# A layer of linear attention and gated MLP: the down projection done by Strassen's method, 7 products for 8

## The chip, the cores and the metric

The kernel runs on one core of a Trainium2 chip. The metric is the device time of one execution in microseconds (us). The profile of an execution has a span about 1.7 us shorter than its device time (792.57 us and 790.9 us for the profiled execution of the kernel before). Where two kernels are compared by time, they are medians; where stages are compared, they are read from the spans of the profiles.

In this text, TensorE is the matrix engine (PE in the profile), PEld its weight loads, VectorE is DVE, ScalarE is ACT, and SP is the engine that issues most DMAs, one after the other, in program order. TensorE's results land in PSUM, in banks (one holds 128 x 512 values here); an *eviction* is the VectorE or ScalarE instruction that reads a finished bank, so that it can be used again. A *residual* is the part of h that is added to the result. The *releaser* of an idle time is what the profile says ended it, and the *granted clock* is the share of the full TensorE clock that the trace records.

## The reference, cut to what matters

```
def reference(A_x, A_wqkv, A_wo, B_x, B_W_gate, B_W_up, B_W_down):
    ...                                   # linear attention block on layernorm(x), 32 heads
    def _B_ref(x, W_gate, W_up, W_down):
        gate = jnp.einsum("bsd,df->bsf", x, W_gate)
        up = jnp.einsum("bsd,df->bsf", x, W_up)
        gate = gate * (gate > 0)
        h = gate * up
        return jnp.einsum("bsf,fd->bsd", h, W_down)
    h = x + _A_ref(_layernorm(x), A_wqkv, A_wo)
    h2 = h + _B_ref(_layernorm(h), B_W_gate, B_W_up, B_W_down)
    return h2
```

2048 tokens (S), width D = 1024, hidden width F = 3584, all bfloat16. The last einsum is the down projection: a 2048 x 3584 matrix times a 3584 x 1024 matrix.

## The kernel before

The MLP is done in two passes of 1024 tokens. In each pass a *gate/up stage* fills `hh` (28 tiles of 128 hidden units x 1024 tokens) and a *down stage* multiplies it by W_down. The gate/up stage already uses the Strassen-Winograd scheme: 14 pairs, each with 7 products for gate and 7 for up, 4 matmuls each, so 56 matmuls per pair where 64 would be needed. For that it forms sums of weight blocks (`t_sums`) and of activation blocks (`s_sums`) on VectorE. The down stage is plain: four rounds of 28 x 4 matmuls.

```
NPASS = 2; TOK = S // NPASS; FTB = 4; NFB = NFT // FTB       # NFT = 28 tiles of F, NFB = 7 chunks
NWS = 4                                                      # W_down ring: 4 chunks of 512 KB
...
def load_wd_next():                                          # next chunk of W_down into the ring
    ...
    rd, c = L // NFB, L % NFB
    dh = rd % ND2
    i = L % NWS
    dma(sl_wd[i], wdring[:, i, :, :], wd_v[:, c * FTB:(c + 1) * FTB, dh * NW:(dh + 1) * NW],
        "ld_wd_%d" % L, writes=[B_wd[i]])
...
def d_round(ps_, hf, dh, banks4, stagger=False, fill=()):    # one round: 512 tokens x 512 columns
    ...
    for j in range(STB):                                     # residuals h, loaded at the round's start
        ...
        dma(sl_hr[k], hres[:, k, :], h_scr[st * P:(st + 1) * P, dh * NW:(dh + 1) * NW], ...)
    def d_mm(ft, j):
        ...
        mm(bank(banks4[j], NW), hh[:, ft, jt * P:(jt + 1) * P], wdring[:, ws, fl, :], ...)
    def d_evac(j):                                           # PSUM + residual -> bf16 -> store
        ...
    for c in range(NFB):
        fts = list(range(c * FTB, (c + 1) * FTB))
        if c == NFB - 1:                                     # last chunk: bank by bank
            for j in range(STB):
                for ft in fts:
                    d_mm(ft, j)
                d_evac(j)
        else:
            for ft in fts:
                for j in range(STB):
                    d_mm(ft, j)
        load_wd_next()
        if fill:
            fill.pop(0)()                                    # pass 0: layernorm of the second half
```

All DMAs, loads and stores alike, are issued by SP in program order (`dma` adds to the program of "sp"). A DMA that must wait for a semaphore therefore holds every DMA behind it.

## Time and profile before

| what | value | view |
|---|---|---|
| device time | 793.66 us median (793.29 to 795.0; 3 runs) | times |
| span | 790.9 us | page |
| TensorE busy | 99%, 3791 matmuls | page, part 1 |
| VectorE busy | 55% | page, part 1 |
| chain that ended last | 95% matmul | page, part 4 |
| down projection | 896 matmuls | groups |

From the page of the kernel before, part 1 (busy time of each engine) and part 4 (the chain that ended last):

```profile
PE 779.6 (99%) x3791; PEld 360.0 (46%) x3791; DVE 434.4 (55%) x900; ACT 237.3 (30%) x394; POOL 30.5 (4%) x60
...
PE 95%; DVE 2%; issue 1%; DMA 1%; SPq 1%; ACT 0%; POOL 0%; DVEq 0%; POOLq 0%
```

The 99% alone is not relied on here: the Trainium skill ("Perfetto Trace Analysis", Identifying the Most-Contended Engine) says that matmul busy time is a poor measure of how close a kernel is to its peak, because matmuls are pipelined. The chain is the stronger evidence: 95% of the span is one matmul after another.

From the groups of instructions of the kernel before, each shape on its own; columns are line, engine, operation, tiles, shapes, count, busy us, mean ns of one, and idle time before with its releaser:

```profile
L504 PE MATMUL ps<-RW,RAB 128*128 128x512 bf16 x896 | 193.9, 380 | 1.1 <-DMA RW<-in_B_W_down_dram 1.1
L777 DVE TENSOR_TENSOR RE<-wring,RE 128x512 f16<-128x512 bf16 x108 | 45.5, 421 | 1.8
L777 DVE TENSOR_TENSOR RE<-wring 128x512 f16<-128x512 bf16 x108 | 40.6, 418 | 0.0
L894 DVE TENSOR_TENSOR RX<-ps,RX 128x512 bf16<-128x512 f32 x32 | 21.8, 690 | 127.3 <-PE ps L504 106.6
L838 DVE TENSOR_TENSOR RAB<-ps,RAB 128x512 bf16<-128x512 f32 x28 | 19.4, 692 | 109.9 <-PE ps L504 109.9
```

The first line is the down projection: 896 matmuls, of which the busy sum of 193.9 us gives 0.216 us each (the 380 ns is from start to end of one, and they overlap). The two L777 lines are what a weight sum of 128 x 512 costs on VectorE, the L894 line what an eviction of one PSUM bank costs. L838 is the first eviction of each gate/up pair: VectorE is idle 3.9 us (109.9 / 28) before it on average. That is the room in which new sums can hide.

The two down stages of the kernel before, in TensorE's timeline (start us, duration us, engine, line, operation, count, idle before and releaser). First pass 0:

```profile
423.74 38.15 PE L504 MATMUL ps<-RW,RAB 128*128 128x512 bf16 x176
463.04 58.94 PE L504 MATMUL ps<-RW,RAB 128*128 128x512 bf16 x272 [1.15 <-DMA RW<-in_B_W_down_dram]
521.81 1.89 PE L504 MATMUL ps<-hnT,wring 128*128 128x512 bf16 x8
...
691.03 96.86 PE L504 MATMUL ps<-RW,RAB 128*128 128x512 bf16 x448
```

Pass 1 (last line) has 448 matmuls in one block: from the first start to the last, 447 steps, it is 96.86 less the last one's 0.38 us, so 0.2158 us each, and 448 of them are 96.69 us. The Trainium skill ("TensorE: Matmul & The Clock Gate", Part 2, Step-by-step) gives 512/2.4 + about 2.5 ns, measured 215.7 ns, from one matmul to the next; this trace has 215.8 ns and agrees. Pass 0 takes 521.81 - 423.74 = 98.07 us, 1.38 us more, because of one gap, shown as 1.15 us. The reason for it is in SP's timeline of the same kernel:

```profile
450.81 2.12 SPq L437 DMA_DIRECT2D out_dram<-RX  x4
453.03 0.39 SPq L437 DMA_DIRECT2D RW<-in_B_W_down_dram  x1
453.52 1.24 SPq L441 DMA_TRANSPOSE hnT<-RE  x1
454.85 0.53 SPq L437 DMA_DIRECT2D RE<-h_scr  x1
455.43 1.92 SPq L437 DMA_DIRECT2D RX<-h_scr  x4
457.44 0.38 SPq L437 DMA_DIRECT2D RW<-in_B_W_down_dram  x1
```

Between two loads of W_down (453.03 and 457.44 us) stand a transpose, a load of the layernorm's input and four loads of residuals, all behind four stores that wait for their evictions. The second of these loads lands 5.55 us after it was issued, just too late, as the chain of waits has it (start us, us, what):

```profile
457.44 5.55 DMA RW<-in_B_W_down_dram
```

That flight is itself longer than the 3.7 us median of the W_down loads of this kernel.

### The profile page before, as it was taken

The numbers are of one execution on the slowest core, as the hardware profiler recorded it, in microseconds if no ns is written. First come the engines' busy times: TensorE is split into PE (matmuls) and PEld (weight loads), VectorE is DVE, ScalarE is ACT, GpSimd is POOL, SyncE is SP. The second block draws the span as 40 slices with busy tenths as digits, with TensorE's granted clock in tenths as the row PEclk, the third lists the DMA queues.
The fourth block names the chain that finished last, engine by engine and source line by source line (L and its number), as shares of the span: only waits on it lengthen the run. The fifth ranks groups of instructions, "written<-read, shape, count | busy, mean of one in ns | idle before, by whom it ended". The sixth has DMA issues, their size and how long they took to land.

```text
span 790.9 us, 10017 instructions
## 1 busy us (share of the span) xinstructions
PE 779.6 (99%) x3791; PEld 360.0 (46%) x3791; DVE 434.4 (55%) x900; ACT 237.3 (30%) x394; POOL 30.5 (4%) x60
## 2 busy tenths in 40 slices
PE   8999999999979999999999999999999999999998
PEld 4444444444434444444444444444444444444443
DVE  7445535799986667576573632145756756501111
ACT  4333333323210544544542000025445454400000
POOL 2000000001500000000000100000000000000000
PEclk9999999999999999999999999999999999999999
DMA  9677400155564532331335997633323222046562
GB/s 314 189 188 180 112 17 1 27 125 146 143 134 123 170 107 62 98 107 54 107 96 170 240 266 238 203 117 106 93 68 106 73 89 80 0 133 204 196 211 81
DMA packets 160128, 102.37 MB, mean 129 GB/s; under 512 B 50384, under 2 KB 153040, under 8 KB 160080
## 3 DMA queue, kind: packets, MB, share of 16 engines
q1 hardware_dynamic: 160080, 101.73, 44.8%
q8 instruction: 30, 0.49, 0.3%
q14 instruction: 18, 0.15, 0.1%
HBM read 81.79 MB, written 8.39 MB: 114 GB/s over the span
## 4 chain that ended last, share of the span: by engine, by line
PE 95%; DVE 2%; issue 1%; DMA 1%; SPq 1%; ACT 0%; POOL 0%; DVEq 0%; POOLq 0%
PE ps L504 95%; DMA RW<-in_B_W_down_dram 1%; DVE RO L679 1%; DVE RC L761 0%; SPq L437 0%; DVE RX L894 0%; PE ps L573 0%; DVE hsb L703 0%; SPq L441 0%; DVE rden L672 0%; DVE dtmp L668 0%; DVE RX L540 0%; ACT RX L538 0%; DVE RAB L543 0%; POOL hsb L399 0%
## 5 line engine op out<-in xcount | busy, mean ns | idle before, releaser
L504 PE MATMUL ps<-RW,RAB 128*128 128x512 bf16 x896 | 193.9, 380 | 1.1 <-DMA RW<-in_B_W_down_dram 1.1
L504 PE MATMUL ps<-RC,RE 128*128 128x512 f16 x672 | 154.2, 380 | 0.0
L504 PEld LDWEIGHTS ps<-RW,RAB 128*128 128x128 bf16 x896 | 87.4, 98 | 107.3 <-DMA RW<-in_B_W_down_dram 1.8
L788 ACT ACTIVATE ps<-ps 128x512 f32<-128x512 f32 x112 | 65.2, 582 | 187.9 <-PE ps L504 187.3
L504 PE MATMUL ps<-RAB 128*128 128x512 bf16 x512 | 113.4, 380 | 0.9 <-ACT RAB L576 0.7
L504 PE MATMUL ps<-hnT,wring 128*128 128x512 bf16 x448 | 105.9, 380 | 0.0
L504 PEld LDWEIGHTS ps<-RC,RE 128*128 128x128 f16 x672 | 65.7, 98 | 79.4
L894 DVE TENSOR_TENSOR RX<-ps,RX 128x512 bf16<-128x512 f32 x32 | 21.8, 690 | 127.3 <-PE ps L504 106.6
L788 ACT ACTIVATE RO<-ps 128x512 f32<-128x512 f32 x112 | 66.9, 597 | 54.5 <-PE ps L504 54.5
L838 DVE TENSOR_TENSOR RAB<-ps,RAB 128x512 bf16<-128x512 f32 x28 | 19.4, 692 | 109.9 <-PE ps L504 109.9
L504 PEld LDWEIGHTS ps<-RAB 128*128 128x128 bf16 x512 | 49.3, 98 | 57.7 <-ACT RAB L576 0.9
L504 PEld LDWEIGHTS ps<-hnT,wring 128*128 128x128 bf16 x448 | 43.8, 98 | 52.9
L538 ACT ACTIVATE RX<-ps 128x512 bf16<-128x512 f32 x64 | 38.0, 594 | 89.1 <-PE ps L504 62.4
L504 PE MATMUL ps<-RW,RO 128*128 128x512 bf16 x256 | 59.2, 387 | 0.4 <-DMA RO<-RO 0.4
L504 PE MATMUL ps<-RAB,RC 128*128 128x512 bf16 x256 | 58.7, 379 | 0.0
L540 DVE TENSOR_SCALAR RX<-RX 128x512 bf16<-128x512 bf16 x64 | 19.5, 305 | 61.3 <-ACT RX L538 61.2
L504 PE MATMUL ps<-hnT,RE 128*128 128x512 bf16 x224 | 52.9, 380 | 0.0
L504 PE MATMUL ps<-RC,wring 128*128 128x512 f16 x224 | 52.9, 380 | 0.0
L788 ACT ACTIVATE RAB<-ps 128x512 bf16<-128x512 f32 x56 | 33.4, 597 | 62.0 <-PE ps L504 62.0
L777 DVE TENSOR_TENSOR RE<-wring,RE 128x512 f16<-128x512 bf16 x108 | 45.5, 421 | 1.8
L845 DVE TENSOR_TENSOR RO<-ps,RO 128x512 f32<-128x512 f32 x56 | 38.7, 692 | 5.5 <-ACT RO L788 5.4
L777 DVE TENSOR_TENSOR RE<-wring 128x512 f16<-128x512 bf16 x108 | 40.6, 418 | 0.0
(59 smaller groups left out, 486.7 us busy)
## 6 DMA issues: line engine op xcount, KB each, us to landing
RW<-in_B_W_down_dram SPq DMA_DIRECT2D x56, 512.0 KB, 3.7
wring<-in_B_W_gate_dram SPq DMA_DIRECT2D x28, 512.0 KB, 3.8
wring<-in_B_W_up_dram SPq DMA_DIRECT2D x28, 512.0 KB, 4.8
RAB<-in_A_wqkv_dram SPq DMA_DIRECT2D x8, 512.0 KB, 7.7
RX<-in_A_x_dram SPq DMA_DIRECT2D x16, 256.0 KB, 3.1
h_scr<-hsb SPq DMA_DIRECT2D x16, 256.0 KB, 3.3
RX<-h_scr SPq DMA_DIRECT2D x32, 128.0 KB, 3.7
out_dram<-RX SPq DMA_DIRECT2D x32, 128.0 KB, 1.7
```

The source lines that it names most:

```text
L504: lambda e: e.matmul(out_ap, lhsT, rhs, start=start, stop=stop, skip_group_check=skip),
L538: PL.add("act", lambda e: e.activation(out=Et[:, k, 0:w], in_=src, func=ACTF.Exp), reads=[B_bank[b]], writes=[B_E[k]], name=name + "_exp")
L540: PL.add("dve", lambda e: e.tensor_scalar(out=E2t[:, k, 0:w], in0=Et[:, k, 0:w], scalar1=1.0, scalar2=1e-6, op0=ALU.min, op1=ALU.add), rea ...
L679: lambda e, nbk=nbk, g0=g0, ng=ng: e.tensor_tensor(out=osb[:, k, g0 * P:(g0 + ng) * P].rearrange("p (g h e) -> p g h e", g=ng, e=Dh), in0= ...
L777: PL.add(eng, lambda e: e.tensor_tensor(out=Tring[:, k, j], in0=in0, in1=in1, op=ALU.subtract), reads=reads, writes=[B_T[k][j]], name="T%d ...
L788: PL.add("act", lambda e: e.activation(out=dst, in_=src, func=func), reads=reads, writes=writes, name=name)
L838: PL.add("dve", lambda e: e.tensor_tensor(out=hh[:, f1, 0:SBW], in0=bank(BA[1]), in1=r11[:, rr, :], op=ALU.mult), reads=[B_bank[BA[1]], B_ ...
L845: PL.add("dve", lambda e, w=w: e.tensor_tensor(out=ftmp[:, 4 + w, :], in0=bank(BF_[w]), in1=ftmp[:, 2 + w, :], op=ALU.add), reads=[B_bank[ ...
L894: PL.add("dve", lambda e: e.tensor_tensor(out=outst[:, k, :], in0=bank(banks4[j], NW), in1=hres[:, k, :], op=ALU.add), reads=[B_bank[banks ...
```

## The change

The intent: do the down stage with the same Strassen-Winograd scheme, 7 products for 8. Call the activations A (rows: two blocks of 512 tokens, t; columns: even and odd tiles of F, k) and the weights B (rows: even and odd tiles of F; columns: the two halves of D). With

- D1 = A10 + A11, D2 = D1 - A00, D3 = A00 - A10, D4 = A01 - D2 (activation sums, FP16),
- T0 = B01 - B00, T1 = B11 - T0, T2 = B11 - B01, T3 = B10 - T1 (weight sums, FP16),

seven products replace eight: C00 = A00 B00 + A01 B10; U = A00 B00 + D2 T1; V = U + D3 T2; C11 = V + D1 T0; C10 = V + A11 T3; C01 = U + D1 T0 + D4 B11.

The weight sums are the same for both passes. They are formed once, by VectorE, during pass 0's gate/up stage, and put into a DRAM scratch (`t_scr`), from which the down stages load them. Most of the activation sums overwrite `hh` in place.

```diff
-    FTB = 4
-    NFB = NFT // FTB
+    FTB = 2
+    NFB = NPAIR // FTB
+    t_scr = nc.dram_tensor("t_scr", [4 * P, NPAIR * NW], f16).ap()
...
-        NWS = 4
+        NWS = 8                       # ring: 8 chunks of 256 KB
+        NHR = 8                       # residual buffers, 4 before
+        NWR = 2
...
+        WSRC = [("b", 0, 0), ("t", 1), ("b", 1, 0), ("t", 2), ("t", 0), ("t", 3), ("b", 1, 1)]
...
+        def wd_sums(q):               # weight sums of pair q, then to DRAM
+            ...
+            add(0, wb(0, 1), wb(0, 0), [B_wraw[k]])
+            add(2, wb(1, 1), wb(0, 1), [B_wraw[k]])
+            add(1, wb(1, 1), wsum[:, k, 0, :], [B_wraw[k], B_wsum[k][0]])
+            add(3, wb(1, 0), wsum[:, k, 1, :], [B_wraw[k], B_wsum[k][1]])
+            if q + NWR < NPAIR:
+                load_wraw(q + NWR)
+            dma(sl_ws[k], t_v[:, :, q, :], wsum[:, k, :, :], "st_wt_%d" % q, ...)
...
+        def down_pass(ps_, fill):
+            XB, YB = [0, 1, 2, 3], [4, 5, 6, 7]          # two sets of four PSUM banks
+            ...
+            seq = [                                      # banks, activations, FP16?, start, eviction
+                (XB, a_hh(0, 0), False, True, e_s1),     # A00 B00
+                (YB, a_16(0, 0), True, True, e_u),       # D2 T1
+                (XB, a_hh(1, 0), False, False, e_11),    # A01 B10
+                (YB, a_16(0, 1), True, True, e_v),       # D3 T2
+                (XB, a_d1(), True, True, e_22),          # D1 T0
+                (YB, a_hh(1, 1), True, True, e_21),      # A11 T3
+                (XB, a_16(1, 0), False, False, e_12),    # D4 B11
+            ]
+            ...                        # 7 chunks per product; in the last chunk bank by bank,
+                                       # 2 matmuls per bank, then evac(j)
+                    if c == 1 and pi in (1, 3, 4, 5):    # residuals load in mid-product
+                        ld_h(...)
+                    if fill and n[0] % 3 == 2:           # late layernorm at every third chunk
+                        fill.pop(0)()
...
+        wt_at = {0: [0], 1: [1, 2], 2: [3, 4]}           # weight sums per gate/up pair of pass 0
+        for q in range(3, 12):
+            wt_at[q] = [q + 2]
```

A caution on the values: the down projection adds at most 0.001 to outputs of standard deviation 0.078 (reckoned by running the reference with W_down set to zero). The comparison with the reference therefore hardly sees the down projection. What speaks for the change's correctness is its algebra, written out above, not that comparison.

More of the change, by code (lines that the diff above doesn't have):

```diff
@@ L189, in bass_sequential_preLN__linear_attn_block__glu_gated_reglu__prompt_kernel @@
     wu_v = B_W_up.rearrange("(dc p) f -> p dc f", p=P)
-    wd_v = B_W_down.rearrange("(ft p) c -> p ft c", p=P)
+    wd_v = B_W_down.rearrange("(q k p) c -> p k q c", k=2, p=P)
+    t_scr = nc.dram_tensor("t_scr", [4 * P, NPAIR * NW], f16).ap()
+    t_v = t_scr.rearrange("(o p) (q c) -> p o q c", p=P, c=NW)
     h_scr = nc.dram_tensor("h_scr", [S, D], bf16).ap()
@@ L221, in bass_sequential_preLN__linear_attn_block__glu_gated_reglu__prompt_kernel @@
         o0 = NFT * TOK
+        hh16 = RAB[:, 0:NFT * TOK].bitcast(f16).rearrange("p (a b) -> p a b", a=NFT)
+        dsum = RAB[:, o0:o0 + 4 * SBW].bitcast(f32).rearrange("p (a b) -> p a b", a=2)
         r11 = RAB[:, o0:o0 + 2 * SBW].rearrange("p (a b) -> p a b", a=2)
@@ L232, in bass_sequential_preLN__linear_attn_block__glu_gated_reglu__prompt_kernel @@
         wdring = RW[:].rearrange("p (s f c) -> p s f c", s=NWS, f=FTB)
+        wdring16 = RW[:].bitcast(f16).rearrange("p (s f c) -> p s f c", s=NWS, f=FTB)
+        wraw = RW[:, 0:NWR * 2 * D].rearrange("p (s k c) -> p s k c", s=NWR, k=2)
+        wsum = RW[:, NWR * 2 * D:NWR * 2 * D + NWR * 4 * NW].bitcast(f16).rearrange("p (s o c) -> p s o c", s=NWR, o=4)
         hnT = sb("hnT", [P, NDC, TOK], bf16)
@@ L253, in bass_sequential_preLN__linear_attn_block__glu_gated_reglu__prompt_kernel @@
         wring = sb("wring", [P, NWG, NDC, 2 * P], bf16)
-        xn = sb("xn", [P, NXN, D], bf16)
-        hsb = sb("hsb", [P, NHS, D], bf16)
+        RXH = sb("RXH", [P, (NXN + NHS) * D], bf16)
+        xn = RXH[:, 0:NXN * D].rearrange("p (a b) -> p a b", a=NXN)
+        hsb = RXH[:, NXN * D:(NXN + NHS) * D].rearrange("p (a b) -> p a b", a=NHS)
+        D1 = RXH[:].bitcast(f16).rearrange("p (q t) -> p q t", t=SBW)
         RX = sb("RX", [P, 2 * NPH * NW + NX2 * D], bf16)
@@ L260, in bass_sequential_preLN__linear_attn_block__glu_gated_reglu__prompt_kernel @@
         x2 = RX[:, o0:o0 + NX2 * D].rearrange("p (a b) -> p a b", a=NX2)
-        hres = RX[:, 0:NOS * NW].rearrange("p (a b) -> p a b", a=NOS)
-        outst = RX[:, NOS * NW:2 * NOS * NW].rearrange("p (a b) -> p a b", a=NOS)
+        hres = RX[:, 0:NHR * NW].rearrange("p (a b) -> p a b", a=NHR)
+        outst = RX[:, NHR * NW:(NHR + NOS) * NW].rearrange("p (a b) -> p a b", a=NOS)
         zeros_t = hsb[:, 0, 0:512]
@@ L303, in bass_sequential_preLN__linear_attn_block__glu_gated_reglu__prompt_kernel @@
         sl_wd = slots("dwd_", NWS)
-        sl_hr = slots("dhr_", NOS)
+        sl_hr = slots("dhr_", NHR)
+        sl_wr = slots("dwr_", NWR)
+        sl_ws = slots("dws_", NWR)
         sl_out = slots("dout_", NOS)
@@ L347, in bass_sequential_preLN__linear_attn_block__glu_gated_reglu__prompt_kernel @@
         B_hh = [bufs("hh%d_" % i, 2) for i in range(NFT)]
-        B_s7 = bufs("s7_", 2)
-        B_sc = bufs("sc_", 2)
-        B_c21 = bufs("c21_", 2)
-        B_c22 = bufs("c22_", 2)
+        B_f = bufs("f_", 8)
+        B_s7, B_sc, B_c22, B_c21 = B_f[0:2], B_f[2:4], B_f[4:6], B_f[6:8]
+        B_U, B_V = B_f[0:4], B_f[4:8]
         B_r11 = bufs("r11_", 2)
         B_r12 = bufs("r12_", 2)
+        B_dsum = [B_r11, B_r12]
         B_wd = bufs("wd_", NWS)
-        B_hres = bufs("hres_", NOS)
+        B_hres = bufs("hres_", NHR)
+        B_wraw = bufs("wraw_", NWR)
+        B_wsum = [bufs("wsum%d_" % i, 4) for i in range(NWR)]
+        B_tscr = bufs("tscr_", NPAIR)
+        B_D1 = bufs("D1_", NPAIR)
         B_outst = bufs("outst_", NOS)
@@ L372, in bass_sequential_preLN__linear_attn_block__glu_gated_reglu__prompt_kernel @@
             b_.over = B_wq
+        for b_ in B_wraw + flat(B_wsum):
+            b_.over = B_wo
         for b_ in B_wd:
-            b_.over = B_wo
-        for b_ in B_s7 + B_sc + B_c21 + B_c22:
+            b_.over = B_wraw + flat(B_wsum)
+        for b_ in B_D1:
+            b_.over = B_xn + B_hs
+        for b_ in B_f:
             b_.over = B_o + B_oT
@@ L487, in bass_sequential_preLN__linear_attn_block__glu_gated_reglu__prompt_kernel, with load_wraw, wb, add @@
         wd_next = [0]
-        NROUND = NPASS * 2 * ND2
+        WSRC = [("b", 0, 0), ("t", 1), ("b", 1, 0), ("t", 2), ("t", 0), ("t", 3), ("b", 1, 1)]
         def load_wd_next():
             L = wd_next[0]
-            if L >= NROUND * NFB:
+            if L >= NPASS * 7 * NFB:
                 return
             wd_next[0] += 1
-            rd, c = L // NFB, L % NFB
-            dh = rd % ND2
             i = L % NWS
-            dma(sl_wd[i], wdring[:, i, :, :], wd_v[:, c * FTB:(c + 1) * FTB, dh * NW:(dh + 1) * NW],
-                "ld_wd_%d" % L, writes=[B_wd[i]])
+            c = L % NFB
+            src = WSRC[(L // NFB) % 7]
+            if src[0] == "b":
+                dma(sl_wd[i], wdring[:, i, :, :],
+                    wd_v[:, src[1], c * FTB:(c + 1) * FTB, src[2] * NW:(src[2] + 1) * NW],
+                    "ld_wd_%d" % L, writes=[B_wd[i]])
+            else:
+                dma(sl_wd[i], wdring16[:, i, :, :], t_v[:, src[1], c * FTB:(c + 1) * FTB, :],
+                    "ld_wt_%d" % L, reads=B_tscr[c * FTB:(c + 1) * FTB], writes=[B_wd[i]])
+        def load_wraw(q):
+            k = q % NWR
+            dma(sl_wr[k], wraw[:, k, :, :], wd_v[:, :, q, :], "ld_wraw_%d" % q, writes=[B_wraw[k]])
+        def wd_sums(q):
+            k = q % NWR
+            def wb(r, h):
+                return wraw[:, k, r, h * NW:(h + 1) * NW]
+            def add(o, in0, in1, reads):
+                PL.add("dve", lambda e: e.tensor_tensor(out=wsum[:, k, o, :], in0=in0, in1=in1, op=ALU.subtract),
+                       reads=reads, writes=[B_wsum[k][o]], name="WT%d_%d" % (o, q))
+            add(0, wb(0, 1), wb(0, 0), [B_wraw[k]])
[4 more added lines that the diff above has]
+                load_wraw(q + NWR)
+            dma(sl_ws[k], t_v[:, :, q, :], wsum[:, k, :, :], "st_wt_%d" % q, reads=B_wsum[k], writes=[B_tscr[q]])
         def mm(out_ap, lhsT, rhs, start, stop, reads, bbuf, name, skip=False):
@@ L788, in ident_act, with hh_sums, strassen_pair @@
             PL.add("act", lambda e: e.activation(out=dst, in_=src, func=func), reads=reads, writes=writes, name=name)
-        def strassen_pair(ps_, q, fill):
+        def hh_sums(q):
+            f1, f2 = 2 * q, 2 * q + 1
+            PL.add("dve", lambda e: e.tensor_tensor(out=D1[:, q, :], in0=hh[:, f1, SBW:2 * SBW],
+                                                    in1=hh[:, f2, SBW:2 * SBW], op=ALU.add),
+                   reads=[B_hh[f1][1], B_hh[f2][1]], writes=[B_D1[q]], name="D1_%d" % q)
+            PL.add("dve", lambda e: e.tensor_tensor(out=hh16[:, f1, SBW:2 * SBW], in0=hh[:, f1, 0:SBW],
+                                                    in1=hh[:, f1, SBW:2 * SBW], op=ALU.subtract),
+                   reads=[B_hh[f1][0]], writes=[B_hh[f1][1]], name="D3_%d" % q)
+        def strassen_pair(ps_, q, fill, mid):
             Lg = (ps_ * NPAIR + q) * 2
@@ L833, in strassen_pair @@
             fillin(2)
+            for f_ in mid:
+                f_()
             for w in range(2):
@@ L868, in strassen_pair, with ld_h, tt, put @@
             load_w_next()
+        hr_ctr = [0]
         os_ctr = [0]
-        def d_round(ps_, hf, dh, banks4, stagger=False, fill=()):
-            rd = (ps_ * 2 + hf) * ND2 + dh
-            kk = []
-            for j in range(STB):
-                st = ps_ * TPP + hf * STB + j
+        U_ = [ftmp[:, j, :] for j in range(STB)]
+        V_ = [ftmp[:, STB + j, :] for j in range(STB)]
+        def down_pass(ps_, fill):
+            XB, YB = [0, 1, 2, 3], [4, 5, 6, 7]
+            hr = {}
+            def ld_h(blk, dh):
+                for j in range(STB):
+                    st = ps_ * TPP + blk * STB + j
+                    k = hr_ctr[0] % NHR
+                    hr_ctr[0] += 1
+                    hr[(blk, dh, j)] = k
+                    dma(sl_hr[k], hres[:, k, :], h_scr[st * P:(st + 1) * P, dh * NW:(dh + 1) * NW],
+                        "ld_h_%d_%d" % (st, dh), reads=[B_hscr[st]], writes=[B_hres[k]])
+            def tt(dst, in0, in1, reads, writes, name, op=ALU.add):
+                PL.add("dve", lambda e: e.tensor_tensor(out=dst, in0=in0, in1=in1, op=op), reads=reads,
+                       writes=writes, name=name)
+            def put(blk, dh, j, in0, in1, reads):
+                st = ps_ * TPP + blk * STB + j
@@ L877, in d_round @@
                 k = os_ctr[0] % NOS
                 os_ctr[0] += 1
-                kk.append(k)
-                dma(sl_hr[k], hres[:, k, :], h_scr[st * P:(st + 1) * P, dh * NW:(dh + 1) * NW],
-                    "ld_h_%d_%d" % (st, dh), reads=[B_hscr[st]], writes=[B_hres[k]])
-            def d_mm(ft, j):
-                c, fl = ft // FTB, ft % FTB
-                ws = (rd * NFB + c) % NWS
-                jt = hf * STB + j
-                mm(bank(banks4[j], NW), hh[:, ft, jt * P:(jt + 1) * P], wdring[:, ws, fl, :],
-                   ft == 0, ft == NFT - 1, [B_hh[ft][hf], B_wd[ws]], B_bank[banks4[j]],
-                   "d_%d_%d" % (rd, ft))
@@ L891, in d_evac @@
-            def d_evac(j):
-                st = ps_ * TPP + hf * STB + j
-                k = kk[j]
-                PL.add("dve", lambda e: e.tensor_tensor(out=outst[:, k, :], in0=bank(banks4[j], NW),
-                                                        in1=hres[:, k, :], op=ALU.add),
-                       reads=[B_bank[banks4[j]], B_hres[k]], writes=[B_outst[k]], name="out_%d_%d" % (st, dh))
+                tt(outst[:, k, :], in0, in1, reads, [B_outst[k]], "out_%d_%d" % (st, dh))
                 dma(sl_out[k], ov[st * P:(st + 1) * P, dh * NW:(dh + 1) * NW], outst[:, k, :],
@@ L898, in d_evac, with hv @@
                     "st_%d_%d" % (st, dh), reads=[B_outst[k]])
-            for c in range(NFB):
-                fts = list(range(c * FTB, (c + 1) * FTB))
-                if c == NFB - 1:
-                    for j in range(STB):
-                        for ft in fts:
-                            d_mm(ft, j)
-                        d_evac(j)
-                else:
-                    for ft in fts:
-                        for j in range(STB):
-                            d_mm(ft, j)
-                load_wd_next()
-                if fill:
-                    fill.pop(0)()
+            def hv(blk, dh, j):
+                k = hr[(blk, dh, j)]
+                return hres[:, k, :], B_hres[k]
@@ new lines, in e_s1, with e_u, e_11, e_v @@
+            def e_s1(j):
+                ident_act(U_[j], bank(XB[j]), [B_bank[XB[j]]], [B_U[j]], "ds1")
+            def e_u(j):
+                tt(U_[j], bank(YB[j]), U_[j], [B_bank[YB[j]]], [B_U[j]], "dU")
+            def e_11(j):
+                h, hb = hv(0, 0, j)
+                put(0, 0, j, bank(XB[j]), h, [B_bank[XB[j]], hb])
+            def e_v(j):
+                tt(V_[j], bank(YB[j]), U_[j], [B_bank[YB[j]], B_U[j]], [B_V[j]], "dV")
+            def e_22(j):
+                h, hb = hv(1, 1, j)
+                k = j % 2
+                tt(dsum[:, k, :], bank(XB[j]), V_[j], [B_bank[XB[j]], B_V[j]], B_dsum[k], "d22")
+                put(1, 1, j, dsum[:, k, :], h, B_dsum[k] + [hb])
@@ new lines, in e_21, with e_12, add_h, a_hh @@
+            def e_21(j):
+                put(1, 0, j, bank(YB[j]), V_[j], [B_bank[YB[j]], B_V[j]])
+            def e_12(j):
+                put(0, 1, j, bank(XB[j]), U_[j], [B_bank[XB[j]], B_U[j]])
+            def add_h(dst, bufs_, blk, dh):
+                for j in range(STB):
+                    h, hb = hv(blk, dh, j)
+                    tt(dst[j], dst[j], h, [hb], [bufs_[j]], "dh")
+            def a_hh(k, t):
+                return (lambda q, j: hh[:, 2 * q + k, (t * STB + j) * P:(t * STB + j + 1) * P]), \
+                       (lambda q: B_hh[2 * q + k][t])
@@ new lines, in a_16, with a_d1, d2, d4 @@
+            def a_16(k, t):
+                return (lambda q, j: hh16[:, 2 * q + k, (t * STB + j) * P:(t * STB + j + 1) * P]), \
+                       (lambda q: B_hh[2 * q + k][t])
+            def a_d1():
+                return (lambda q, j: D1[:, q, j * P:(j + 1) * P]), (lambda q: B_D1[q])
+            def d2(q):
+                tt(hh16[:, 2 * q, 0:SBW], D1[:, q, :], hh[:, 2 * q, 0:SBW], [B_D1[q]], [B_hh[2 * q][0]],
+                   "D2_%d" % q, op=ALU.subtract)
+            def d4(q):
+                tt(hh16[:, 2 * q + 1, 0:SBW], hh[:, 2 * q + 1, 0:SBW], hh16[:, 2 * q, 0:SBW], [B_hh[2 * q][0]],
+                   [B_hh[2 * q + 1][0]], "D4_%d" % q, op=ALU.subtract)
@@ new lines, in down_pass, with d_mm @@
+            seq = [
[7 more added lines that the diff above has]
+            ]
+            n = [0]
+            for pi, (bk, (af, ab), w16, start, evac) in enumerate(seq):
+                for c in range(NFB):
+                    ws = ((ps_ * 7 + pi) * NFB + c) % NWS
+                    wr = wdring16 if w16 else wdring
+                    last = c == NFB - 1
+                    def d_mm(fl, j):
+                        q = c * FTB + fl
+                        mm(bank(bk[j]), af(q, j), wr[:, ws, fl, :], start and q == 0, q == NPAIR - 1,
+                           [ab(q), B_wd[ws]], B_bank[bk[j]], "d%d_%d_%d" % (pi, ps_, q), skip=True)
+                    if last:
+                        for j in range(STB):
+                            for fl in range(FTB):
+                                d_mm(fl, j)
+                            evac(j)
+                    else:
+                        for fl in range(FTB):
+                            for j in range(STB):
+                                d_mm(fl, j)
+                    load_wd_next()
+                    if pi == 0:
+                        d2(2 * c)
+                        d2(2 * c + 1)
+                    if pi == 2 and c >= 1:
+                        d4(2 * c - 2)
+                        d4(2 * c - 1)
+                    if pi == 3 and c == 0:
+                        d4(2 * NFB - 2)
+                        d4(2 * NFB - 1)
+                    if c == 1 and pi in (1, 3, 4, 5):
+                        ld_h(*{1: (0, 0), 3: (1, 1), 4: (1, 0), 5: (0, 1)}[pi])
+                    if pi == 5 and c == 2:
+                        add_h(V_, B_V, 1, 0)
+                    if pi == 6 and c == 2:
+                        add_h(U_, B_U, 0, 1)
+                    if fill and n[0] % 3 == 2:
+                        fill.pop(0)()
+                    n[0] += 1
@@ L1005, in bass_sequential_preLN__linear_attn_block__glu_gated_reglu__prompt_kernel @@
                 s_sums()
-        for _ in range(NWS):
-            load_wd_next()
+        for q in range(NWR):
+            load_wraw(q)
+        wt_at = {0: [0], 1: [1, 2], 2: [3, 4]}
+        for q in range(3, 12):
+            wt_at[q] = [q + 2]
         for p_ in range(NPASS):
@@ L1014, in bass_sequential_preLN__linear_attn_block__glu_gated_reglu__prompt_kernel @@
                     fill = fill + t_sums(nxt) + t_sums(nxt + 1)
-                strassen_pair(p_, q, fill)
-                assert not fill or q == NPAIR - 1 or len(fill) <= 0
-            rounds = [(hf, dh) for hf in range(2) for dh in range(ND2)]
-            for i, (hf, dh) in enumerate(rounds):
-                late = []
-                if p_ + 1 < NPASS and i < 2:
-                    for t in range(i * NFB, (i + 1) * NFB):
-                        late.append(lambda t=t: late_ln(t))
-                if p_ + 1 < NPASS and i == 2:
-                    late.append(s_sums)
-                d_round(p_, hf, dh, [0, 1, 2, 3] if i % 2 == 0 else [4, 5, 6, 7], fill=late)
-                assert not late
+                if q > 0:
+                    hh_sums(q - 1)
+                mid = []
+                if p_ == 0:
+                    for x in wt_at.get(q, []):
+                        mid.append(lambda x=x: wd_sums(x))
+                strassen_pair(p_, q, fill, mid)
+                if p_ == 0 and q == 12:
+                    for _ in range(NWS):
+                        load_wd_next()
+            assert not fill
+            hh_sums(NPAIR - 1)
+            late = []
+            if p_ + 1 < NPASS:
+                for t in range(TPP + 2):
+                    late.append(lambda t=t: late_ln(t))
+                late.append(s_sums)
+            down_pass(p_, late)
+            assert not late
         PL.finalize(eng_sems)
```

## The prediction

> **What bounds the kernel now.** TensorE. The page's part 1 has it busy 99% of a 790.9 us span, the chain that ended last is 95% matmul, and the granted clock is 0.998. In the second pass's down projection (timeline of TensorE, 691.03 us on) 448 matmuls follow each other without a gap and end at 787.7 us: 96.7 us, so 0.216 us each (the groups' 380 ns is pipelined latency). The Trainium skill ("VectorE: DVE Perf Modes", the TRN2 errata) gives 215 ns for a 512-column matmul; this trace agrees. VectorE is busy 55%.
>
> **Removed.** The down projection has 896 matmuls (group RW,RAB). Seven products for eight leave 784: 112 fewer, 112 x 0.216 = 24.2 us, all critical, 12.1 us per pass. Gate/up products on FP16 sums already run at this pitch. Also removed is a 1.15 us TensorE gap at 463 us (queue held by residual loads, W_down tile late); residuals now have twice the buffers and load mid-product.
>
> **Added, mostly hidden.**
> - Weight sums, 14 x 4 VectorE ops of 128x512 to FP16. The gate/up weight sums of this shape take 418 to 421 ns, so 1.7 us per pair, in pass 0 only. Activation sums: 4 per pair and pass at about 0.42 us, half of them in the gate/up stage (0.84 us per pair). A pair takes 12.1 us (56 matmuls); VectorE idles about 3.8 us of it before its first eviction (line 838: 53.6 us idle over 14 pairs). 0.84 + 1.7 = 2.5 us fits. Pairs 1 and 2 carry two sets (4.2 us), overrunning by about 0.4 us; the bank they delay is next needed over 5 us later.
> - Evictions in the down stage: about 28 FP32 ops from PSUM or SBUF at 0.69 us plus 8 residual adds per pass, some 25 us, and 12 us of in-place sums, in 84.6 us. Products alternate between two sets of four banks, so each eviction has a 12 us window. No wait expected.
> - DMA: ring loads keep their rate (256 KB per 1.73 us against 512 KB per 3.46 us); 14 raw loads and 14 stores of 512 KB are new, in pass 0.
>
> **What I expect to be given back.**
> - Pass 0, about 1.5 us: the layernorm of the second half ends later in the down stage; its sums (4 x 1.22 us) wait for the last transpose (4.5 us in flight) and come just before the longest eviction, 8 x 0.69 us (product 5). Its stores stand in the DMA queue ahead of the weight loads. I reckon the queue blocked some 9 us against a ring of 8 chunks (13.8 us) and 4 us of flight, so the first tile of product 7 lands 1 to 2 us late.
> - Tail, 0.7 us: the last chunk gives 0.43 us of matmuls per bank (0.86 before), less than one 0.69 us eviction, so evictions queue after the last matmul.
>
> **Sum.** 793.7 - 24.2 - 1.2 + 1.5 + 0.7 = 770.5 us. Range 767.5 to 774.5. Faster by over 2% (below 777.8): 0.94; within 2%: 0.05; slower: 0.01.
>
> **What would show it.** 784 matmuls in the down groups at an unchanged 0.216 us pitch; pass 1's down stage 84.6 us without gaps; pass 0's at 86 us with its one gap before product 7, released by a W_down or scratch DMA; gate/up stages still 12.1 us per pair; VectorE about 65% busy.
>
> **What would make it wrong.** Weight sums pushing VectorE late enough to hold gate/up banks (pairs over 12.1 us); a longer or repeated stall of the DMA queue in the down stage; a lower granted clock.

## More of the kernel before

(Idle time counts from the end of a matmul, 0.38 us after its start, when the next could have started 0.16 us earlier; so a gap costs about 0.16 us more than it shows.)

## The result and the profile after

| | before | after |
|---|---|---|
| device time, median | 793.47 us (791.29 to 795.0, 4 runs) | 768.12 us (767.77 to 768.56, 4 runs) |
| ratio after to before | | 0.968, 95% interval 0.966 to 0.971: faster |
| span of the profile | 790.9 us | 766.2 us |

The 793.47 us are the three runs from above and a fourth of 791.29 us. A ratio is the mean time of one kernel's fast runs over that of the other's of the same rounds, so it is not quite the ratio of the medians quoted.

From the page of the changed kernel, parts 1 and 4:

```profile
PE 751.8 (98%) x3615; PEld 349.6 (46%) x3679; DVE 519.6 (68%) x1108; ACT 241.4 (32%) x402; POOL 30.6 (4%) x60
...
PE 95%; DVE 3%; issue 1%; ACT 1%; DVEq 0%; POOL 0%; ACTq 0%; POOLq 0%
```

The bound has not moved. The weight loads are 3679, exactly 112 fewer than 3791. (The matmul records show 3615; this trace lacks some of them, so the weight loads are the count to use.) VectorE does 208 more operations.

The changed kernel's TensorE timeline, down stage of pass 0, then of pass 1:

```profile
423.88 48.51 PE L553 MATMUL ps<-RW,RAB 128*128 128x512 bf16 x221
472.23 12.25 PE L553 MATMUL ps<-RW,RXH 128*128 128x512 f16 x56
484.31 12.25 PE L553 MATMUL ps<-RW,RAB 128*128 128x512 f16 x56
496.90 12.03 PE L553 MATMUL ps<-RW,RAB 128*128 128x512 bf16 x54 [0.34 <-DVE RX L949]
508.77 1.89 PE L553 MATMUL ps<-hnT,wring 128*128 128x512 bf16 x8
...
677.99 48.51 PE L553 MATMUL ps<-RW,RAB 128*128 128x512 bf16 x221
726.33 12.25 PE L553 MATMUL ps<-RW,RXH 128*128 128x512 f16 x56
738.42 24.34 PE L553 MATMUL ps<-RW,RAB 128*128 128x512 f16 x110
```

Products follow each other at 12.08 to 12.09 us (472.23 to 484.31, 726.33 to 738.42), which is 56 x 0.2158, whatever their types. Pass 1 has no gap. Pass 0 has one before product 7. It is shown as 0.34 us, but two of product 7's 56 records are missing (x54), the first among them; the stage loses 84.89 - 392 x 0.2158 = 0.28 us (unrounded).

Putting the boundaries of the stages of both spans side by side (each is the start of the first matmul of the next stage) shows where the 24.6 us came from (the last two rows with the unrounded spans):

| stage | before, us | after, us | saved |
|---|---|---|---|
| attention, up to the first gate/up matmul | 254.53 | 254.67 | -0.14 |
| gate/up, pass 0 | 169.21 | 169.21 | 0.00 |
| down, pass 0 | 98.07 | 84.89 | 13.18 |
| gate/up, pass 1 | 169.22 | 169.22 | 0.00 |
| down, pass 1, with the tail | 99.83 | 88.25 | 11.58 |
| span | 790.86 | 766.24 | 24.62 |

The gate/up stage of pass 0, which now carries all weight sums and half of the activation sums, has not grown by a hundredth of a microsecond. The gate/up and down stages of pass 0 by windows, for the busy time of each engine (columns: window, its length, then busy us and count of PE, PEld, DVE, ACT, POOL, then granted clock, DMA share and GB/s). Before:

```profile
254.50:423.70 169.20, 169.20 (x785) 76.65 (x784) 111.48 (x224) 82.74 (x140) 0.00 (x0) 1.00 0.32 95
423.70:521.80 98.10, 96.95 (x449) 43.66 (x448) 33.05 (x61) 0.00 (x0) 4.39 (x8) 1.00 0.82 237
```

After:

```profile
254.60:423.90 169.30, 168.56 (x773) 76.73 (x785) 141.10 (x306) 82.75 (x140) 0.00 (x0) 1.00 0.59 182
423.90:508.80 84.90, 84.35 (x389) 38.31 (x393) 54.67 (x110) 2.07 (x4) 4.58 (x8) 1.00 0.88 250
```

In pass 0's gate/up stage VectorE went from 111.5 to 141.1 us of 169.2, and the DMA engines from 32% to 59%. Both are still off the critical path. The margin is thin in the pairs with two sets of weight sums. The pairs 1 and 2 of the changed kernel, and then a pair with one set:

```profile
267.00:279.00 12.00, 11.95 (x56) 5.46 (x56) 11.76 (x28) 5.91 (x10) 0.00 (x0) 1.00 0.76 239
279.20:291.30 12.10, 12.05 (x57) 5.47 (x56) 11.72 (x27) 5.91 (x10) 0.00 (x0) 1.00 0.86 269
...
303.40:315.50 12.10, 12.05 (x56) 5.49 (x56) 10.17 (x23) 5.91 (x10) 0.00 (x0) 1.00 0.58 175
```

VectorE is busy 11.7 to 11.8 us of some 12 in the first two, 10.2 in the third (the kernel before: 7.9 to 8.0 in each).

The gap before product 7: VectorE's timeline of the changed kernel first, then SP's.

```profile
482.78 2.36 DVE L810 TENSOR_TENSOR RC<-hnT 128x2048 f16<-128x2048 bf16 x2 [3.95 <-DMA hnT<-RE]
485.18 1.23 DVE L810 TENSOR_TENSOR RC<-RC,hnT 128x2048 f16<-128x2048 f16 x1
486.44 1.23 DVE L810 TENSOR_TENSOR RC<-hnT,RC 128x2048 f16<-128x2048 bf16 x1
487.58 0.68 DVE L949 TENSOR_TENSOR RAB<-ps,RO 128x512 f32<-128x512 f32 x1
```

```profile
478.91 1.24 SPq L463 DMA_TRANSPOSE hnT<-RE  x1
480.25 2.90 SPq L459 DMA_DIRECT2D RW<-t_scr  x4
489.07 4.48 SPq L459 DMA_DIRECT2D out_dram<-RX  x4
493.65 1.45 SPq L459 DMA_DIRECT2D RW<-in_B_W_down_dram  x3
```

VectorE waits 3.95 us for the last transpose of the late layernorm, then does the four sums (L810) before it can evict product 5 (from 487.58 us on). Product 5's four stores stand in SP's program ahead of the next weight load. SP has issued its last load at 483.15 us (480.25 + 2.90) and issues the next one only at 493.65 us. That one is the first chunk of product 7, which TensorE wants at 496.4 us. The profile puts the gap down to an eviction (`DVE RX L949`). The eviction running at that moment is product 6's, and no operand or bank of product 7 depends on it, so I took it for a late tile; experiments e3 and e4 decide. The kept trace of this run says so too: the tile landed 2.9 us after its issue, at 496.55 us, and TensorE's queue holds a wait for that load's semaphore which ended at 496.58 us. TensorE's instructions after it wait for VectorE's semaphore as well, and the first matmul's record is missing, which may be why the profile named VectorE. In e5, e6, e7 and e9, which have the same queue, that wait also ended 0.03 us after the tile's landing.

### The profile page after: what moved, and what is told of

It reads as the page before. It is cut to its first block, busy times and chain, and to the rows that moved or that the text cites. A ratio compares the mean times of both kernels' runs of the same rounds, so it can differ in the third digit from the quotient of the medians.

```text
span 766.2 us, 10114 instructions
## 1 busy us (share of the span) xinstructions
PE 751.8 (98%) x3615; PEld 349.6 (46%) x3679; DVE 519.6 (68%) x1108; ACT 241.4 (32%) x402; POOL 30.6 (4%) x60
## 4 chain that ended last, share of the span: by engine, by line
PE 95%; DVE 3%; issue 1%; ACT 1%; DVEq 0%; POOL 0%; ACTq 0%; POOLq 0%
PE ps L553 94%; ACT RX L587 1%; DVE RAB L592 1%; DVE RO L728 1%; DVE RC L810 0%; DVE RX L589 0%; DVE RX L949 0%; PE ps L622 0%; DVE RXH L752 0%; DVE rden L721 0%; DVE dtmp L717 0%; DVE RE L592 0%; DVEq L1187 0%; POOL RXH L421 0%; ACT RAB L625 0%
## 5 line engine op out<-in xcount | busy, mean ns | idle before, releaser
L553 PE MATMUL ps<-RW,RAB 128*128 128x512 f16 (+1 forms) x662 | 145.2, 379 | 0.8 <-DVE RX L949 0.3
L553 PEld LDWEIGHTS ps<-RW,RAB 128*128 128x128 bf16 (+1 forms) x672 | 65.7, 98 | 79.7 <-DVE RX L949 0.6
L837 ACT ACTIVATE RO<-ps 128x512 f32<-128x512 f32 x120 | 71.0, 597 | 76.7 <-PE ps L553 54.5
L553 PE MATMUL ps<-hnT,RE 128*128 128x512 bf16 x196 | 47.0, 379 | 1.5
L553 PEld LDWEIGHTS ps<-RW,RO 128*128 128x128 bf16 x256 | 25.2, 99 | 30.8 <-issue 2.3
```

What stands on the lines that cost most here:

```text
L553: lambda e: e.matmul(out_ap, lhsT, rhs, start=start, stop=stop, skip_group_check=skip),
L837: PL.add("act", lambda e: e.activation(out=dst, in_=src, func=func), reads=reads, writes=writes, name=name)
```

## Experiments

Twelve kernels were run. "Queue edit" below means that the output stores are issued from ScalarE's DMA queue.

### e1: an eighth product put back

```diff
-        WSRC = [..., ("t", 3), ("b", 1, 1)]
+        WSRC = [..., ("t", 3), ("b", 1, 1), ("b", 1, 1)]
...
-                (XB, a_16(1, 0), False, False, e_12),
+                (XB, a_16(1, 0), False, False, None),
+                (XB, a_16(1, 0), False, False, e_12),
```

Its output is wrong, which doesn't matter for the time. Product 7 is done twice, so the matmul count is that of the kernel before.

> An eighth product is put back: product 7 runs twice in each pass (wrong values, same matmul count, 896, as the kernel before; everything else as changed). Theory (the gain is the matmul count, the rest nets to about nothing): 768.1 + 112 x 0.216 = 792.3 us, within about 1.5 us of the kernel before (793.5). Rival (a good part of the 25 us came from something else, such as the reordered queue or other banks): it stays well under 790 us, and the second pass's down stage shows it.

Measured: 792.43 us (791.12 to 794.59), the kernel before in the same rounds 793.05 us; ratio 1.000, interval 0.998 to 1.002: the same. What the change saves is its 112 matmuls; everything else that it adds, moves and repairs nets to nothing within that interval of 0.2% (1.6 us). (e1 has gaps of its own before and within the added products: its down stage of pass 0 takes 98.45 us, 1.8 us over 448 x 0.2158.)

### e2 to e4: the gap before product 7

e2 does the second half's activation sums twice, which makes VectorE later by about 4.8 us at the crucial place and changes nothing else:

```diff
-                late.append(s_sums)
+                late.append(lambda: (s_sums(), s_sums()))
```

> The activation sums of the second half (4 VectorE ops, 4.9 us), which stand before product 5's eviction in pass 0, are done twice (result unchanged). Theory: VectorE's lateness holds the stores, the stores hold the DMA queue, and the weight tile for product 7 is late by the same 4.9 us: the gap before product 7 grows from 0.35 to about 5.2 us, and the time to about 773.0 us. Rival (the slot was luck, there is slack of several us left): under 770 us.

e3 is the queue edit; e4 is both edits together.

```diff
-            return PL.add("sp", lambda e: e.dma_start(dst_ap, src_ap), ...)
+            return PL.add(eng, lambda e: e.dma_start(dst_ap, src_ap), ...)
...
-                    "st_%d_%d" % (st, dh), reads=[B_outst[k]])
+                    "st_%d_%d" % (st, dh), reads=[B_outst[k]], eng="act")
```

> The output stores are issued from ScalarE's DMA queue instead of the common one, so that weight loads no longer stand behind them. Theory (the gap of 0.35 us before product 7 is a late weight tile): the gap goes, about 767.8 us. Rival (the gap is what the profile names, a wait for VectorE's eviction): the gap stays at 0.35 us and the time at 768.1.

> Both edits: sums twice and stores on ScalarE's queue. VectorE is as late as with the sums twice alone, but the weight loads are free. Late-tile theory: no gap before product 7, about 767.8 us. Rival (VectorE holds TensorE directly, through a bank or an operand): about 5 us of gap and 773 us, as without the queue edit.

| | median, us | down stage of pass 0 in the profile, us (84.6 without a gap) |
|---|---|---|
| changed kernel | 768.12 | 84.89 |
| e2, sums twice | 774.86 (772.96 to 775.44) | 90.92 |
| e3, queue edit | 767.52 (767.19 to 767.78) | 84.60 |
| e4, both | 767.47 (767.32 to 768.6) | 84.75 |

The gap of e2 in TensorE's timeline:

```profile
500.30 13.64 PE L553 MATMUL ps<-RW,RAB 128*128 128x512 bf16 x56 [4.76 <-DMA RW<-in_B_W_down_dram]
```

and its chain of waits just before that (start us, us, what):

```profile
496.19 0.70 DVE RX L949
496.89 0.02 issue
496.91 0.33 SPq L459
...
497.34 2.82 DMA RW<-in_B_W_down_dram
500.16 0.14 issue
500.30 4.79 PE ps L553 x15
```

Here the chain is plain: the last eviction, the last store's issue, the weight load and its 2.82 us of flight, the matmul. With the queue edit TensorE's timeline of e4 shows no gap:

```profile
483.79 24.48 PE L553 MATMUL ps<-RW,RAB 128*128 128x512 f16 x112
```

In e4 VectorE is as late as in e2 (product 5's eviction begins at 491.64 us, more than 7 us after the product's end), and TensorE's stage loses 0.14 us where e2's loses 6.3. So it was not VectorE that held TensorE directly in e2; the late tile did, by way of the queue, and the releaser that the profile named in the changed kernel was not the cause. The 0.14 us show the limits of this. 0.12 us of it is a weight load at 501.19 us that waits for the fourth chunk of product 7: its DMA still stood in SP's queue behind residual loads, which the queue edit leaves there and which wait for VectorE. And 0.02 us is a direct wait: product 7 adds to the banks that product 5's evictions read, and the first matmul into the fourth bank started at 496.53 us, just after that read ended (496.47). VectorE much later than in e4 would hold TensorE directly. e2's time came out 1.9 us above the expected 773.0: the profiled execution had 772.96 us at a granted clock of 0.996, and the others, at 0.990 to 0.993, took 774.55 to 775.44. The gap itself is 4.76 us against 5.2 expected. The stage lost more than its gap, 90.92 - 84.6 = 6.3 us: after the gap matmuls start 0.43 us apart until 502.8 us, at a granted clock of 0.50 in that window, so that the 15 of the chain's last line take 4.79 us in place of about 3.4. Whether the queue edit alone is worth anything in time, e3 does not settle: its gain of 0.6 us in the median is from another job than the run of the changed kernel, and the repeat e9 below has 767.32 us.

### e5 and e10: without the weight sums

```diff
...
-        WSRC = [("b", 0, 0), ("t", 1), ("b", 1, 0), ("t", 2), ("t", 0), ("t", 3), ("b", 1, 1)]
+        WSRC = [("b", 0, 0), ("b", 0, 1), ("b", 1, 0), ("b", 0, 0), ("b", 0, 1), ("b", 1, 0), ("b", 1, 1)]
...
-        for q in range(NWR):
-            load_wraw(q)
-        wt_at = {0: [0], 1: [1, 2], 2: [3, 4]}
-        ...
+        wt_at = {}
...
-                    wr = wdring16 if w16 else wdring
+                    wr = wdring
```

No weight sums, no raw loads, no scratch; plain tiles in their place. Their outputs are wrong, which doesn't matter for the times.

> The weight sums, their 14 raw loads and 14 scratch stores are taken away; every product reads plain W_down tiles instead (wrong values, same matmuls, same ring sizes). Theory (the preparation is hidden): 768.1 us within 0.3. Rival (it costs through VectorE or DMA contention): 1 us or more faster.

Measured: 770.36 us (769.03 to 771.95), *slower* by about 2 us than the changed kernel. This contradicted both theories. The profile shows that the edit touched something else: gate/up of pass 0 takes 169.21 us, as with the sums, but the down stage of pass 0 takes 86.29 us, with a gap of 1.52 us before product 7, released by a W_down load. In this run the last transpose was issued 0.9 us later in its stage and flew 0.5 us longer (VectorE waited 4.44 us for it, 3.95 in the changed kernel), the sums began 1.4 us later (60.3 us into the stage against 58.9), and all behind it, up to that weight load, was late by as much. Why the transpose was later with plain tiles I did not follow further. Part of the extra time in the other rounds is a lower clock (0.993 in the slowest). So e10 repeats the removal with the queue edit, which takes the held queue out:

> Weight sums, raw loads and scratch stores taken away as in the run without preparation, but with the stores on ScalarE's queue, so that the gap before product 7, which in that run had grown to 1.5 us, cannot blur the reading (wrong values). Theory (preparation is hidden): 767.5 us, as the run with that queue edit alone, within 0.3. Rival (preparation costs): 766.5 or less. Rival (reading plain tiles is slower for another reason than the held queue): above 769.

Measured: 767.35 us (766.92 to 768.72); gate/up of pass 0 169.21 us, down stage of pass 0 84.61 us. The same as with the weight sums (e3: 767.52 us, 169.22 us, 84.60 us; e9, the unedited kernel in e10's own job: 767.32 us). The preparation is free as it stands.

### e6 and e7: the weight sums two and three times

```diff
+            for _ in range(2):          # e7: range(3)
+                add(0, ...); add(2, ...); add(1, ...); add(3, ...)
```

How far is it from not being free?

> Each set of weight sums is computed twice (result unchanged): 1.5 us more VectorE work per set. A pair with one set then needs 10.2 + 1.5 = 11.7 us of VectorE in 12.1 us and still fits; pairs 1 and 2 with two sets need 11.75 + 3.0 = 14.8 us and run 2.7 us late each. My reckoning of the banks' slack is about 4 us, against a lateness of 2.4 + 2.6 + 2.6 = 7.6 us: TensorE should lose about 3.5 us there and nothing later: 771.6 us. Rival (slack is larger, all hidden): 768.1. Rival (preparation is on the path): 14 x 1.5 = 21 us more.

> Each set three times: a pair with one set needs 10.2 + 3.1 = 13.3 us of VectorE in 12.1 us, so VectorE becomes the bound of the first 12 pairs of pass 0: about 1.2 us per pair for nine pairs and 12 us or so in pairs 0 to 2, less 4 us of slack: about 786 us (783 to 790). The rival with large slack: under 775.

| | median, us | gate/up of pass 0, us | expected there |
|---|---|---|---|
| changed kernel | 768.12 | 169.21 | |
| e6, twice | 772.46 (771.7 to 772.78) | 172.65 (+3.4) | +3.5 |
| e7, three times | 787.91 (787.22 to 788.54) | 188.54 (+19.3) | +18 |

In TensorE's timeline of e7 the loss comes first in two large steps and then in every pair:

```profile
284.26 1.89 PE L554 MATMUL ps<-hnT,wring 128*128 128x512 bf16 x4 [4.21 <-DVE RAB L899]
...
301.69 1.04 PE L554 MATMUL ps<-hnT,wring 128*128 128x512 bf16 x4 [2.25 <-DVE RAB L899]
303.07 2.85 PE L554 MATMUL ps<-RC,RE 128*128 128x512 f16 x12 [0.35 <-DVE RO L906]
...
316.10 2.84 PE L554 MATMUL ps<-RC,RE 128*128 128x512 f16 x12 [0.35 <-DVE RO L906]
```

From pair 3 on, a pair takes 13.03 us (303.07 to 316.10) in place of 12.09: VectorE is the bound. This makes the hiding a measured margin: one more set in a single-set pair fits, and two more do not; and about 4 us of lateness is swallowed by the banks before TensorE stops (an estimate: the 7.6 us of lateness reckoned for e6 less the 3.4 us lost). e7's 19.3 us are not all VectorE's work: after its 4.21 us gap 15 matmuls start 0.43 us apart, at a granted clock of 0.50, as in e2. Both runs also lost about 1 us more in the down stage of pass 0 (85.78 and 86.08 us), by the same late tile and, in e7, a second one later in product 7.

### e8: the queue edit on the kernel before

> The kernel before, with its output stores and residual loads of the down stage moved to ScalarE's DMA queue. Theory (its 1.15 us gap in pass 0 is the queue held by them, and the change's better queue order accounts for about 1 us of the 25): about 792.3 us and no gap in pass 0's down stage. Rival: 793.5 and the gap stays.

The stores and the residual loads of the down stage go to ScalarE's queue. Measured: 792.22 us (791.38 to 795.4) against 792.9 us; ratio 0.9986, interval 0.9966 to 1.0006, so the gain in time is not settled. The trace is clear: no gap, and the down stage of pass 0 takes 96.82 us where it took 98.07:

```profile
423.77 96.98 PE L504 MATMUL ps<-RW,RAB 128*128 128x512 bf16 x439
```

The load that came late in the kernel before is issued 2.9 us earlier (454.50 us) and lands 1.2 us earlier (461.83 us in the kept trace). Which of the two, stores or residual loads, held it was not tried apart. Of the change's 24.6 us in the span, about 1 us (1.38 us of loss before, 0.28 after) is this repair and not the method.

### e9, e11, e12: the changed kernel again, its tail, and both repairs

e9 is the changed kernel unedited, in the same job as e10, e11 and e12.

> The changed kernel once more, unedited, so that the three below are compared with it on the same chip in the same rounds: 768.1 us, with a gap of 0.3 to 0.4 us before product 7 of pass 0.

e11 does the last two chunks of the last product bank by bank, so that a bank gets four matmuls before its eviction:

```diff
-                    def d_mm(fl, j):
+                    def d_mm(fl, j, c=c):
...
+                    end = pi == 6 and ps_ == NPASS - 1
-                    if last:
+                    if end and c == NFB - 2:
+                        pass
+                    elif last:
                         for j in range(STB):
+                            if end:
+                                for fl in range(FTB):
+                                    d_mm(fl, j, c - 1)
                             for fl in range(FTB):
                                 d_mm(fl, j)
                             evac(j)
```

> In the last product of the last pass the last two chunks are done bank by bank, four matmuls per bank (0.86 us) ahead of each eviction, as in the kernel before. Theory (evictions of 0.69 us queue after the last matmul because a bank gets only 0.43 us): the span's tail after the last matmul falls from 3.6 to about 3.0 us, about 767.5 us. Rival (the tail is the store's flight): no change.

> Stores on ScalarE's queue and the bank-by-bank end together, result unchanged: 768.1 - 0.4 - 0.6 = about 767.0 us, faster than both kernels.

The last evictions of the changed kernel:

```profile
761.55 2.48 DVE L949 TENSOR_TENSOR RX<-ps,RO 128x512 bf16<-128x512 f32 x4 [7.20 <-issue]
```

and the last two of e11:

```profile
761.47 0.69 DVE L949 TENSOR_TENSOR RX<-ps,RO 128x512 bf16<-128x512 f32 x1 [0.17 <-PE ps L553]
762.33 0.69 DVE L949 TENSOR_TENSOR RX<-ps,RO 128x512 bf16<-128x512 f32 x1 [0.17 <-PE ps L553]
```

Four evictions in one block became evictions that each wait 0.17 us for TensorE, that is, none queues any more.

| | median, us | down stage, pass 0 | tail after the last matmul |
|---|---|---|---|
| e9, unedited | 767.32 (765.98 to 768.28, 5 runs) | 84.75 | 3.65 |
| e11, tail | 767.08 (766.75 to 767.58) | 85.33 | 3.16 |
| e12, both repairs | 766.94 (766.63 to 767.52) | 84.61 | 3.17 |

The tail is the unrounded span less the start of pass 1's down stage less 392 x 0.2158 us. It falls by 0.5 us to what the kernel before has (790.86 - 691.03 - 96.69 = 3.14 us). e9 had almost no gap in its profiled execution, e11 had one of 0.36 us in mid-product 7: without the queue edit the tile and TensorE arrive in a dead heat, and which wins changes from run to run. In time the three can't be told apart: the ranges overlap, and e9's fastest run, at a granted clock of 1.000, is the fastest of all. e12 (ratio to the kernel before 0.967) beats the kernel before as clearly as the change does; that it beats the change is shown by the trace's stages, 0.6 us, and not by the times.

## Why the prediction was right

The prediction, 770.5 us with a range of 767.5 to 774.5, holds the measured 768.12. Point by point:

- **24.2 us from 112 fewer matmuls, all critical: right.** 392 matmuls at 0.2158 us in pass 1's down stage, without a gap; e1, with the count put back, is as slow as the kernel before.
- **FP16 operands at no cost: right.** Products of bf16, FP16 and both kinds mixed all take 12.09 us.
- **Weight and activation sums hidden: right.** Gate/up of pass 0 took 169.21 us before and after; e10 shows no gain when the weight sums are taken away. The margin is also about as reckoned: +3.4 us for +3.5 in e6, and +19.3 us for +18 in e7, part of it the slower matmuls after e7's first gap, which were not reckoned. VectorE is busy 68% (65% said).
- **One gap in pass 0, before product 7, by a held DMA queue: right in place and cause, too large in size.** Said: 1.5 us. The stage lost 0.28 us. As they stand, the prediction's figures do not give its 1.5 us, nor any gap: 9 us of held queue and 4 us of flight are 13 us, less than the ring's 13.8. Measured, the hold was longer, 10.5 us (from 483.15 us to 493.65 us), and the flight shorter, 2.9 us in place of 4 (I had the 3.7 us median of 512 KB loads; this one is 256 KB). The sum, 13.4 us, just exceeds the 13.25 us from 483.15 us to when TensorE wanted the tile, and 0.13 us more pass between the landing and the first matmul. Two errors nearly cancel, so that there was a gap at all is in part luck. The other profiles with the unedited queue show the stage losing from 0.14 us (e9) to 0.7 (e11) and, where VectorE or the transpose was later, 1.2 to 1.7 us (e6, e5), so 1.5 us was a possible outcome and not the likely one.
- **"released by a W_down or scratch DMA": the profile of the changed kernel named VectorE instead.** e2, e3 and e4 show that it was the DMA, and the wait for the load's semaphore in the trace agrees.
- **The old gap of 1.15 us gone: right**, and e8 shows its cause by removing it from the kernel before.
- **Tail +0.7 us: right in kind.** 3.65 us against 3.14 is +0.51 us.

The sum came out 2.4 us too high. The gap's size is 1.22 us of it and the tail's 0.19. The rest is no larger than the 1.1 us by which my starting number, the median of 793.66 us, lay above the profiled execution of 792.57 us from which the durations came, and the kernel before scatters from 791.1 to 796.7 us over all its runs.

## What to carry to other kernels

A method that trades TensorE products for VectorE sums pays its full matmul count where TensorE is the bound and VectorE's idle time lies *where the sums have to be made*: count VectorE's busy time per pair or stage and not over the span, and measure the margin by doing the added work twice and three times. When stores wait for evictions in the same program-ordered queue as the loads, a late eviction becomes a late load, so compare the longest pause between two issues of the critical load with the depth of its ring. A named releaser is a hint: an edit that frees the suspected queue and leaves the named engine just as late settles it. A gap can also cost more than its length: after the 4.76 us gap of e2 the next matmuls ran at half pace and lost another 1.4 us.

## What the Trainium skill lacked or had wrong

- "DMA: Bandwidth & Descriptors", Issuing engines are not separate DMA queues, says that issuing DMAs from several engines "will only save the time on the sequencer it takes to initiate the DMA, which is usually small relative to the DMA itself". Here moving the output stores to ScalarE's queue took away a gap of 4.76 us (e2 against e4) and not for bandwidth: the pause is the sequencer's wait for a semaphore ahead of a load that could go. The same page says, in Anatomy of one DMA (written for the gpsimd path), that any semaphore wait happens on the issuing sequencer before dispatch; this case agrees for SP (it issued nothing from 483.2 to 489.07 us), but the page doesn't draw the consequence for the loads behind. The nearest advice, in "Perfetto Trace Analysis", DMA Optimizations, is to give inputs and outputs an issuing engine each; it gives neither this reason nor a number.
- "Perfetto Trace Analysis", Identifying Dependency Chains, advises reading the semaphores that an instruction waits on. Followed here, it points the right way (TensorE's wait for the load's semaphore, ended at 496.58 us). What it lacks is a warning that a releaser inferred by a tool can be a bystander when matmul records are missing (54 of 56): the gap was put down to a VectorE eviction, and e4 shows VectorE several us later with 0.14 us lost.
- No page tells of trading products for sums. This case: 56 matmuls saved per pass, 12.1 us, against 1.5 us of VectorE per set of four 128 x 512 sums; free up to 11.7 us of VectorE per 12.1 us pair, and 13.03 us per pair with the sums done three times.
